# Linear attention, Fourier mixing and feed-forward on one core: work emitted batch by batch with ranks, against one fixed software pipeline

## The chip, the cores and the metric

The kernel runs on one core of a Trainium2 chip. The metric is device time in microseconds of one launch, and lower is better. Of each version several runs are timed; one more execution is recorded by the profiler, and the views of the profile come from it.

## The reference

Inputs are `r`, `k`, `v` of 4 batches x 8 heads x 768 positions x 48 (float32), a decay `w` and a bonus `u` of 8 x 48, and two feed-forward weights of 384 x 1536 and 1536 x 384. The first half is a linear attention with a decaying state, the second a Fourier mixing with a feed-forward layer:

```python
for t in range(S):
    cur = np.einsum('bhd,bhe->bhde', u[None] * kt, vt)
    y[:, :, t] = np.einsum('bhd,bhde->bhe', rt, state + cur)
    state = w[None, :, :, None] * state + np.einsum('bhd,bhe->bhde', kt, vt)
...
X = np.fft.fft(np.fft.fft(x, axis=1), axis=2)      # x: y with the heads side by side, 4 x 768 x 384
u = x + np.real(X)
un = (u - mean(u)) / np.sqrt(var(u) + 1e-06)       # over the last axis
out = u + np.maximum(un @ w_ch1, 0.0) @ w_ch2
```

## The kernel before, in words

The 768 positions of a batch are cut into 6 chunks of 128 positions, so there are 24 chunks. A batch goes through three functions.

`attention(b, ins)` (L181) runs the 6 chunks of a batch. For each chunk VectorE multiplies keys and queries by powers of the decay into `KR` (L191), ScalarE casts the values to `V` (L196), TensorE transposes `KR` in eight parts into PSUM (`tp`, L202), ScalarE copies that to `KRT` (L204), and VectorE makes the product `PR` (L206). TensorE then makes the 128 x 128 scores of all heads into two PSUM tiles `A_ps` (L212). The first is masked by VectorE (L218), the second is cast by ScalarE (L222) and masked by GpSimd (L223). `yd_ps` collects the output: a bonus per head (L229), the old state (L233), and scores times values (L243); ScalarE copies the bonus (L236), GpSimd multiplies it with `V` (`TT`, L238), and VectorE adds both into `X` (L255). The state is carried from chunk to chunk: TensorE makes `u_ps` (L248, L251), VectorE multiplies it by the decay into `Sst` (L253). After the chunks `fold` (L263) makes sums and differences of the batch's two halves on VectorE (`EO`, `XF`).

`fourier(b, X, XF)` (L271) does the transform over the positions with tables in 18 matmuls (L280), copied out by ScalarE (L282), and a mirrored copy `TR` on VectorE (L285). Then, for each of two halves of 384 positions and each of three blocks, six matmuls with `hid_t` make the second transform (L299, L301, L303); VectorE adds `X` (`UF`, L305) and takes the statistics (L308, L309). Per half ScalarE makes the root (L311) and the normalised `UN` (L318), and a transposing DMA on SP's queue writes `UNT` (L320), which is the input of the feed-forward layer.

`mlp(b, sh, UF, UNT)` (L325) does the feed-forward layer of one half: 12 groups of three matmuls with `W1` (L330), each cast by a ReLU on ScalarE into `HT` (L332), then three groups of 12 matmuls with `W2` (L336), to which VectorE adds `UF` (L339); GpSimd's queue writes the result out (L341). Over the program L330 and L336 have 288 matmuls each. Fourier and feed-forward share three PSUM buffers named `mm`.

What sets the order: the functions are Python that emits instructions; a planner then gives each engine a list, taking at each point of its own estimated time the ready instruction of best rank, and the engine runs this list. Rank is the order of emission, except that what stands in the `tc.high_priority(offset=5000)` block of the last loop (L350) is ranked 5000 places earlier. In that block stand the Fourier of batch `b`, the attention of batch `b + 1` and the loads of batch `b + 2`; the feed-forward of batch `b - 1` is emitted behind it at ordinary rank. The planner also hands out the buffers, and puts in the waits. `sp(...)` (L162) keeps an instruction behind everything emitted before it on its engine, and all loads and transposes of SP's queue go through it, so SP's queue has the order of emission: the loads of batch 0, the tables, the loads of batch 1, the two transposes of batch 0, the loads of batch 2, the transposes of batch 1, and so on. A load of a chunk is three DMAs of 192 KB (L171, L172, L175); the input pool holds 6 chunks. The weights are six DMAs on GpSimd's queue (L154, L156), put behind the `TT` of chunk 2 by `issue_after`.

Of the kernel before, what the change touches and what calls it, by code (L numbers as in the profile page):

```python
# [15 lines left out]
B = 4  # L16
H = 8
# [45 lines left out]
def kernel(  # L63
# [62 lines left out]
    NB = 3  # L126
# [24 lines left out]
    def load_weights():  # L151
        with tc.issue_after(marks["tt2"].ins):
            for dt in range(3):
                nc.gpsimd.dma_start(out=W1[:, dt, :], in_=w1[dt * 128:(dt + 1) * 128, :])  # L154
            for fg in range(3):
                nc.gpsimd.dma_start(out=W2[:, fg * 4:(fg + 1) * 4, :],  # L156
                                    in_=w2[fg * 512:(fg + 1) * 512, :].rearrange("(f p) d -> p f d", p=128))

    count = [0]
# [5 lines left out]
    def loads(b):  # L165
        ins = []
        for q in range(NQ):
            sl = slice(q * 128, (q + 1) * 128)
            kr = inp.tile([128, 2, H, D], F32, name="kr")
            vt = inp.tile([128, H, D], F32, name="vt")  # L170
            sp(nc.sync.dma_start(out=kr[:, 0], in_=k[b, :, sl, :].rearrange("h p d -> p h d")))  # L171
            sp(nc.sync.dma_start(out=kr[:, 1], in_=r[b, :, sl, :].rearrange("h p d -> p h d")))  # L172
            if b == 0 and q == 0:
                sp(nc.sync.dma_start(out=ident, in_=id_c.ap()))
            sp(nc.sync.dma_start(out=vt, in_=v[b, :, sl, :].rearrange("h p d -> p h d")))  # L175
            if b == 0 and q == 0:
                sp(nc.sync.dma_start(out=mtri, in_=mtri_c.ap()))
            ins.append((kr, vt))
        return ins

    def attention(b, ins):  # L181
        X = bp.tile([128, NQ, DM], BF16, name="X")
        EO = bp.tile([128, 2, 3, DM], BF16, name="EO", bufs=1)
        XF = bp.tile([128, 2, 3, DM], BF16, name="XF")
        Sst = None
        for q in range(NQ):
            i = count[0]
            count[0] += 1
            kr, vt = ins[q]
            KR = KRs[i % NB]  # L190
            nc.vector.tensor_tensor(  # L191
                out=KR.rearrange("t s p (a d) -> t (s p) a d", a=2)[:, :, :, 0:D],
                in0=kr.rearrange("t s (p a) d -> t (s p) a d", a=2),
                in1=wtab.rearrange("t s (p a d) -> t (s p) a d", a=2, d=D), op=AluOp.mult)
            V = wp.tile([128, H, D], BF16, name="V")
            cv = nc.scalar.copy(V, vt)  # L196
            if i == 0:
                tc.keep_in_program_order(cv)
            tp = ps.tile([128, 2, NP, 128], BF16, name="tp", bufs=1)
            for s in range(2):  # L200
                for p in range(NP):
                    nc.tensor.transpose(tp[:, s, p, :], KR[:, s, p, :], ident)  # L202
            KRT = wp.tile([128, 2, NP, 128], BF16, name="KRT")
            nc.scalar.copy(KRT, tp)  # L204
            PR = wp.tile([128, NP, 128], BF16, name="PR")
            nc.vector.tensor_tensor(out=PR, in0=KRT[:, 0], in1=KRT[:, 1], op=AluOp.mult)  # L206

            A_ps = [ps.tile([128, NP, 128], F32, name="A_ps", bufs=2) for _ in range(2)]
            for p in range(NP):
                for a in range(2):  # L210
                    rows = slice(a * 64, a * 64 + 64)
                    nc.tensor.matmul(A_ps[a][:, p, :], lhsT=KRT[rows, 0, p, :], rhs=KRT[rows, 1, p, :],  # L212
                                     start=(p == 0), stop=(p == NP - 1), skip_group_check=True)
            MAs = []
            for a in range(2):
                MA = wp.tile([128, NP, 128], BF16, name="MA", bufs=6)
                if a == 0:
                    nc.vector.tensor_tensor(out=MA, in0=A_ps[a], in1=mtri.unsqueeze(1).to_broadcast([128, NP, 128]),  # L218
                                            op=AluOp.mult)
                else:  # L220
                    AC = wp.tile([128, NP, 128], BF16, name="AC", bufs=2)
                    nc.scalar.copy(AC, A_ps[a])  # L222
                    nc.gpsimd.affine_select(out=MA, in_=AC, pattern=[[0, NP], [1, 128]], base=0,  # L223
                                            channel_multiplier=-1, compare_op=AluOp.is_gt, fill=0.0)
                MAs.append(MA)
            yd_ps = ps.tile([128, DM + H], F32, name="yd_ps", bufs=1)
            y_ps = yd_ps[:, 0:DM].rearrange("t (h d) -> t h d", h=H)
            for p in range(NP):
                nc.tensor.matmul(yd_ps[:, DM + 2 * p:DM + 2 * p + 2], lhsT=PR[:, p, :], rhs=UW[:, p, :],  # L229
                                 start=(p == 0), stop=False, skip_group_check=True)  # L230
# [26 lines left out]
            if b == 0 and q >= 3:  # L257
                fold(X, EO, XF, q - 3, q - 2)
# [131 lines left out]
```

## Time and profile before

| | us |
|---|---|
| median of 3 runs (lowest, highest) | 245.33 (243.44, 245.98) |
| profiled execution, its own time | 246.25 |
| its span, first to last instruction | 244.5 |
| TensorE busy (PE) | 192.5 |
| VectorE busy (DVE) | 131.8 |
| ScalarE busy (ACT) | 128.5 |
| GpSimd busy (POOL) | 59.8 |

The DMA queues moved 25.33 MB, of which the queue of SP's loads 17.96 MB. Times in the views are microseconds from the start of the span. PE is TensorE's matmuls, PEld its weight loads, SPq and POOLq the queues of SyncE and GpSimd. A row of a timeline has the start, the length, the engine, the line of the kernel, the operation, the tile written and those read, and how often; in brackets stands the idle time ahead of it and what ended that. The granted clock is the share of TensorE's full clock. "x24" is a count.

### The profile page before, as it was taken

Reading aid. Unit: us, or ns where it says so; the run is one execution under the profiler, and the core shown is the slowest. Engines: PE = TensorE matmul, PEld = TensorE weight load, DVE = VectorE, ACT = ScalarE, POOL = GpSimd, SP = SyncE. Lnnn points to the kernel's source line nnn. Section 1 sums busy time; section 2 is a strip of 40 time slices with the busy share of each in tenths; the row PEclk is TensorE's granted clock in tenths of the full one; section 3 lists DMA queues with packets and bytes.
Section 4 is the critical chain, followed back from the end, with each engine's and each line's share of the span. In section 5 each row is a group of like instructions: output and inputs, shape, how many; then the busy total and the mean of one; then the engine's idle time right before and its main releaser. Section 6 shows DMA issues by size and latency. Waiting matters only on the chain.

```text
span 244.5 us, 4268 instructions
## 1 busy us (share of the span) xinstructions
PE 192.5 (79%) x1640; PEld 122.4 (50%) x1640; DVE 131.8 (54%) x278; ACT 128.5 (53%) x255; POOL 59.8 (24%) x87
## 2 busy tenths in 40 slices
PE   0369760892869579987889899879999699999991
PEld 0256530471657466644555555446656356566560
DVE  3488970689878889693477686802028401011010
ACT  4646510547676445469278824590842955453620
POOL 4046740013233454020154430002010001010111
PEclk9999999998575555999999999999999999999999
DMA  6999999998699900005999200051010322020101
GB/s 115 186 186 214 249 189 192 183 186 121 122 191 171 165 4 0 1 3 99 215 229 190 46 32 35 12 117 64 35 66 0 82 49 97 3 97 31 67 35 64
DMA packets 88917, 25.33 MB, mean 104 GB/s; under 512 B 85312, under 2 KB 86976, under 8 KB 88896
## 3 DMA queue, kind: packets, MB, share of 16 engines
q1 hardware_dynamic: 85216, 17.96, 45.5%
q0 software_dynamic: 3680, 7.08, 11.1%
q8 instruction: 13, 0.21, 0.4%
q14 instruction: 8, 0.07, 0.1%
HBM read 20.32 MB, written 4.72 MB: 102 GB/s over the span
## 4 chain that ended last, share of the span: by engine, by line
issue 39%; PE 18%; DMA 11%; DVE 11%; POOL 8%; ACT 7%; SPq 4%; POOLq 0%; ACTq 0%; DVEq 0%
DMA kr<-in_r_dram 11%; POOL out_dram L341 4%; PE tp L202 4%; DVE KR L191 3%; PE A_ps L212 3%; POOL TT L238 3%; PE mm L280 2%; DVE PR L206 2%; ACT KRT L204 2%; ACT UN L318 1%; ACT HT L332 1%; PE u_ps L248 1%; POOL MA L223 1%; DVE MA L218 1%; PE mm L330 1%
## 5 line engine op out<-in xcount | busy, mean ns | idle before, releaser
L332 ACT ACTIVATE HT<-mm 128x384 bf16<-128x384 f32 x96 | 45.2, 490 | 25.2 <-PE mm L330 25.1
L330 PE MATMUL mm<-UNT,W 128*128 128x384 bf16 x288 | 52.3, 326 | 7.3 <-ACT HT L332 5.3
L336 PE MATMUL mm<-W,HT 128*128 128x384 bf16 x288 | 51.6, 326 | 0.0
L339 DVE TENSOR_TENSOR osb<-mm,UF 128x384 f32<-128x384 f32 x24 | 13.3, 553 | 64.4 <-PE mm L336 64.4
L330 PEld LDWEIGHTS <-W 128*128 128x128 bf16 x288 | 27.5, 98 | 26.1 <-issue 9.5
L202 PE MATMUL tp<-ident,KR 128*128 128x128 bf16 x192 | 22.6, 280 | 21.5 <-DVE KR L191 21.5
L341 POOL DMA_DIRECT2D out_dram<-osb x24 | 13.1, 548 | 100.1 <-DVE osb L339 100.1
L336 PEld LDWEIGHTS <-HT 128*128 128x128 bf16 x288 | 27.7, 98 | 16.9
L191 DVE TENSOR_TENSOR KR<-kr,wtab 128x768 bf16<-128x768 f32 x24 | 26.4, 1099 | 16.1 <-DMA kr<-in_r_dram 16.1
L223 POOL TENSOR_SCALAR_AFFINE_SELECT MA<-AC 128x512 bf16<-128x512 bf16 x24 | 17.2, 718 | 56.5 <-ACT AC L222 27.8
L202 PEld LDWEIGHTS <-KR 128*128 128x128 bf16 x192 | 16.4, 127 | 26.5 <-DVE KR L191 25.5
L204 ACT COPY KRT<-tp 128x1024 bf16<-128x1024 bf16 x24 | 24.3, 1012 | 9.9 <-PE tp L202 9.7
L238 POOL TENSOR_TENSOR TT<-V,DE 128x384 bf16<-128x384 bf16 x24 | 23.2, 968 | 23.3 <-ACT DE L236 23.2
L222 ACT CAST AC<-A_ps 128x512 bf16<-128x512 f32 x24 | 14.1, 586 | 18.7 <-PE A_ps L212 18.7
L196 ACT CAST V<-vt 128x384 bf16<-128x384 f32 x24 | 12.2, 511 | 18.5 <-DMA vt<-in_v_dram 17.9
L282 ACT CAST TT<-mm 128x386 bf16<-128x386 f32 (+1 forms) x24 | 13.4, 596 | 12.3 <-PE mm L280 11.9
L212 PE MATMUL A_ps<-KRT 64*128 64x128 bf16 x192 | 15.5, 270 | 4.5 <-ACT KRT L204 4.1
L255 DVE TENSOR_TENSOR X<-yd_ps,TT 128x384 bf16<-128x384 f32 x24 | 13.2, 550 | 9.5 <-POOL TT L238 8.1
L218 DVE TENSOR_TENSOR MA<-A_ps,mtri 128x512 bf16<-128x512 f32 x24 | 16.3, 682 | 0.7 <-PE A_ps L212 0.6
L318 ACT ACTIVATE UN<-UF,nm,rstd 128x384 bf16<-128x384 f32 x24 | 15.2, 701 | 1.9 <-DVE nm L314 1.9
L212 PEld LDWEIGHTS <-KRT 64*128 64x128 bf16 x192 | 8.4, 113 | 12.0 <-ACT KRT L204 9.4
L243 PE MATMUL yd_ps<-V,MA 128*128 128x48 bf16 x192 | 11.3, 202 | 3.6 <-POOL MA L223 1.2
(64 smaller groups left out, 236.1 us busy)
## 6 DMA issues: line engine op xcount, KB each, us to landing
kr<-in_k_dram SPq DMA_DIRECT2D x24, 192.0 KB, 4.5
kr<-in_r_dram SPq DMA_DIRECT2D x24, 192.0 KB, 4.6
vt<-in_v_dram SPq DMA_DIRECT2D x24, 192.0 KB, 4.6
out_dram<-osb POOLq DMA_DIRECT2D x24, 192.0 KB, 2.1
W<-in_moe_w_ch_dram POOLq DMA_DIRECT2D x6, 384.0 KB, 9.9
hid_t<-hid_c SPq DMA_DIRECT2D x1, 576.0 KB, 7.7
te_t<-te_c SPq DMA_DIRECT2D x1, 289.5 KB, 4.5
to_t<-to_c SPq DMA_DIRECT2D x1, 288.0 KB, 4.1
```

The costliest lines, as they stand in the source:

```text
L191: nc.vector.tensor_tensor(out=KR.rearrange("t s p (a d) -> t (s p) a d", a=2)[:, :, :, 0:D], in0=kr.rearrange("t s (p a) d -> t (s p) a d" ...
L202: nc.tensor.transpose(tp[:, s, p, :], KR[:, s, p, :], ident)
L204: nc.scalar.copy(KRT, tp)
L212: nc.tensor.matmul(A_ps[a][:, p, :], lhsT=KRT[rows, 0, p, :], rhs=KRT[rows, 1, p, :], start=(p == 0), stop=(p == NP - 1), skip_group_check ...
L218: nc.vector.tensor_tensor(out=MA, in0=A_ps[a], in1=mtri.unsqueeze(1).to_broadcast([128, NP, 128]), op=AluOp.mult)
L223: nc.gpsimd.affine_select(out=MA, in_=AC, pattern=[[0, NP], [1, 128]], base=0, channel_multiplier=-1, compare_op=AluOp.is_gt, fill=0.0)
L238: marks["tt%d" % i] = nc.gpsimd.tensor_tensor(out=TT, in0=V, in1=DE.unsqueeze(2).to_broadcast([128, H, D]), op=AluOp.mult)
L318: nc.scalar.activation(out=UN[:, j, :], in_=UF[:, j, :], func=Act.Identity, scale=rstd[:, j:j + 1], bias=nm[:, j:j + 1])
L330: nc.tensor.matmul(hp, lhsT=W1[:, dt, ft * 128:(ft + 1) * 128], rhs=UNT[:, :, dt, :], start=(dt == 0), stop=(dt == 2))
L332: nc.scalar.activation(out=HT[:, ft, :], in_=hp, func=Act.Relu)
L336: nc.tensor.matmul(op, lhsT=HT[:, ft, j * 128:(j + 1) * 128], rhs=W2[:, ft, :], start=(ft == 0), stop=(ft == 11))
L341: nc.gpsimd.dma_start(out=out[b, row:row + 128, :], in_=osb)
```

## The change: what it does

The three functions are cut into pieces that a single loop over steps emits, at ordinary rank everywhere; the rank is thus the order of this loop. Attention of a chunk becomes `phase1` (KR, V, transposes, KRT, PR), `phase2` (scores, masks, the state) and `phase3` (the output, `TT`, `X`, `fold`), and step `s` emits phase 1 of chunk `s`, phase 2 of chunk `s - 1`, phase 3 of chunk `s - 2`. `fourier` becomes a generator that yields after each of its six transform groups and after each of its six blocks; it is advanced three times a step, by three pieces each while `s < 12` and by one after that. The feed-forward work is a list `M` of 120 pieces (`mlp1`: one group of three matmuls and its ReLU; `mlp2`: twelve matmuls and an output), of which each step from `s = 10` on takes 2, 2 and 1, as far as the half that the next piece reads has been emitted. When the chunks are done the last Fourier pieces alternate with single feed-forward pieces, and the rest of `M` follows.

Besides: the loads are emitted one chunk a step, four chunks ahead, six of them at the start; W1 goes behind the `TT` of chunk 2 and W2 behind that of chunk 6; in batch 0 both masks go by ScalarE and GpSimd; the groups of the first transform go by column block outside and parity inside, with the mirrored copy behind each block; there are 4 `KR` buffers (3 before), 4 of `V`, `KRT`, `PR` and `Sst` (3 before), and 5 of `UF` and `UNT` (6 before).

```diff
-    NB = 3
+    NB = 4
...
-    def load_weights():
-        with tc.issue_after(marks["tt2"].ins):
+    def load_w1():
+        with tc.issue_after(marks[2].ins):
             for dt in range(3):
                 nc.gpsimd.dma_start(out=W1[:, dt, :], in_=w1[dt * 128:(dt + 1) * 128, :])
+
+    def load_w2():
+        with tc.issue_after(marks[6].ins):
             for fg in range(3):
...
-                if a == 0:
+            if a == 0 and b > 0:
...
-        for par in range(2):
-            for cb in range(3):
+        for cb in range(3):
+            for par in range(2):
...
+                yield
             nc.vector.tensor_copy(TR[:, cb, :, :], TT[:, cb, :, 384:0:-1])
...
-            UF = bp.tile([128, 3, DM], F32, name="UF", bufs=6)
-            UNT = bp.tile([128, 3, 3, 128], BF16, name="UNT", bufs=6)
+            UF = bp.tile([128, 3, DM], F32, name="UF", bufs=5)
+            UNT = bp.tile([128, 3, 3, 128], BF16, name="UNT", bufs=5)
...
+                if j < 2:
+                    yield
...
-            halves.append((UF, UNT))
-        return halves
+            bat[b]["halves"].append((UF, UNT))
+            yield
...
+    M = []
+    for hf in range(2 * B + 1):
         for j in range(3):
+            if hf < 2 * B:
+                M += [(mlp1, hf, ft) for ft in range(4 * j, 4 * j + 4)]
+            if hf > 0:
+                M += [(mlp2, hf - 1, j)]
+
+    def feed(n):
+        for _ in range(n):
+            if M and len(bat[min(M[0][1] // 2, B - 1)].get("halves", [])) > M[0][1] % 2:
+                f, hf, j = M.pop(0)
+                f(hf, j)
+
+    def advance(g, n):
+        for _ in range(n):
+            if next(g, "end") == "end":
+                return False
+        return True
+
+    INP = 6
+    for i in range(INP):
+        load(i)
     load_tables()
-    xs = [attention(0, ins)]
-    load_weights()
-    ins = loads(1)
-    hs = []
-    for b in range(B + 1):
-        with tc.high_priority(offset=5000):
-            if b < B:
-                hs.append(fourier(b, *xs[b]))
-            if b + 1 < B:
-                xs.append(attention(b + 1, ins))
-            if b + 2 < B:
-                ins = loads(b + 2)
-        if b > 0:
-            for sh in range(2):
-                mlp(b - 1, sh, *hs[b - 1][sh])
+    FG = None
+    MSTART = 10
+    for s in range(NC + 2):
+        if s < NC:
+            phase1(s)
+        if INP <= s + INP - 2 < NC:
+            load(s + INP - 2)
+        if FG:
+            FG = FG if advance(FG, 3 if s < 12 else 1) else None
+        if s >= MSTART:
+            feed(2)
+        if 1 <= s < NC + 1:
+            phase2(s - 1)
+        if FG:
+            FG = FG if advance(FG, 3 if s < 12 else 1) else None
+        if s >= MSTART:
+            feed(2)
+        if s >= 2:
+            phase3(s - 2)
+            if s - 2 == 2:
+                load_w1()
+            if s - 2 == 6:
+                load_w2()
+        if FG:
+            FG = FG if advance(FG, 3 if s < 12 else 1) else None
+        if s >= MSTART:
+            feed(1)
+        if s >= 2 and (s - 2) % NQ == NQ - 1:
+            FG = fourier((s - 2) // NQ)
+    while FG:
+        FG = FG if advance(FG, 1) else None
+        feed(1)
+    feed(len(M))
```

More of the change, by code (lines that the diff above doesn't have):

```diff
@@ L163, in sp @@
         return tc.keep_in_program_order(ins)
[L165 to L208, printed above, removed]
-            for p in range(NP):
[L210 to L214, printed above, removed]
-            for a in range(2):
-                MA = wp.tile([128, NP, 128], BF16, name="MA", bufs=6)
-                if a == 0:
[L218 to L227, printed above, removed]
```

184 lines of the change are left out of this document (128 added, 56 removed).

## The prediction

> **What bounds the kernel now.** First the page: totals and the row of the granted clock.
>
> ```profile
> span 244.5 us, 4268 instructions
> PE 192.5 (79%) x1640; PEld 122.4 (50%) x1640; DVE 131.8 (54%) x278; ACT 128.5 (53%) x255; POOL 59.8 (24%) x87
> ...
> PEclk9999999998575555999999999999999999999999
> ```
>
> TensorE is the busiest engine with 192.5 us, yet 52 us of the span it stands, and for six or seven slices (61 to 98 us) it runs at half its clock. Which stages those are, the view by stretches tells (columns: length, busy time and count of PE, PEld, DVE, ACT, POOL, then granted clock, DMA share, GB/s).
>
> ```profile
> 14.00:44.00 30.00, 17.34 (x188) 11.88 (x186) 20.75 (x36) 10.57 (x20) 13.87 (x18) 1.00 1.19 204
> ...
> 56.00:60.00 4.00, 1.13 (x24) 0.80 (x24) 3.89 (x12) 3.11 (x8) 1.46 (x2) 0.95 0.62 85
> 60.00:64.00 4.00, 2.49 (x20) 1.66 (x22) 3.63 (x6) 3.31 (x5) 0.00 (x0) 0.50 0.41 78
> ...
> 72.00:98.00 26.00, 20.32 (x231) 15.52 (x231) 22.31 (x35) 13.89 (x27) 11.73 (x14) 0.54 0.58 90
> ...
> 118.00:144.00 26.00, 23.29 (x286) 14.05 (x285) 18.28 (x32) 17.57 (x36) 11.81 (x16) 1.00 0.83 146
> 144.00:200.00 56.00, 50.60 (x320) 29.89 (x319) 23.05 (x63) 31.23 (x64) 4.73 (x9) 1.00 0.20 54
> 200.00:239.30 39.30, 39.29 (x242) 23.45 (x240) 6.12 (x11) 17.38 (x36) 5.94 (x11) 1.00 0.14 51
> ```
>
> There are four stages. From 14 to 44 us the DMA engines are full (share 1.19) and PE works 17 of 30 us. From 56 to 98 us attention runs alone, at a clock of 0.5. From 118 us PE has feed-forward work beside attention (23.29 of 26 busy). The last 39.3 us are 242 feed-forward matmuls and nothing else, 39.3 / 242 = 0.1624 us each. The 576 of the whole program (288 each of L330 and L336) are so worth 93.6 us, and the question is when the first of them runs. The timeline of PE says it, and gives durations:
>
> ```profile
> 44.02 1.03 PE L202 MATMUL tp<-ident,KR 128*128 128x128 bf16 x8 [8.78 <-DVE KR L191]
> ...
> 46.70 2.92 PE L280 MATMUL mm<-to_t,XF 128*128 128x384 bf16 x9
> ...
> 99.43 1.62 PE L280 MATMUL mm<-to_t,XF 128*128 128x384 bf16 x9
> ...
> 101.25 0.34 PE L299 MATMUL mm<-hid_t,TT 128*128 128x384 bf16 x1
> ...
> 103.23 0.33 PE L299 MATMUL mm<-hid_t,TR 128*128 128x384 bf16 x1
> ...
> 105.73 0.49 PE L330 MATMUL mm<-UNT,W 128*128 128x384 bf16 x2
> ...
> 120.17 0.62 PE L202 MATMUL tp<-ident,KR 128*128 128x128 bf16 x8 [0.74 <-DVE KR L191]
> ```
>
> Feed-forward starts at 105.73 us. Why so late? The timeline of SP's queue and the DMA list (last column: us to landing) show that its input was there long before:
>
> ```profile
> 49.41 0.94 SPq L171 DMA_DIRECT2D kr<-in_k_dram  x1
> ...
> 52.50 0.96 SPq L171 DMA_DIRECT2D kr<-in_k_dram  x1
> ...
> 58.87 5.26 SPq L320 DMA_TRANSPOSE UNT<-UN  x2
> ...
> 81.80 0.91 SPq L175 DMA_DIRECT2D vt<-in_v_dram  x1
> ...
> 109.86 4.78 SPq L320 DMA_TRANSPOSE UNT<-UN  x2
> ```
>
> ```profile
> UNT<-UN SPq DMA_TRANSPOSE x8, 3.3
> ```
>
> The first transpose of batch 0 is issued at 58.87 and lands 3.3 us later, at about 62. So some 43 us pass in which the feed-forward of batch 0 could fill the holes of attention and doesn't; it stands behind batch 1's Fourier in PE's order. Also, SP issues no load from 82.7 to 114.6: the loads of batch 3 stand behind batch 1's transposes.
>
> **The change, part by part.** I take the time as: start of feed-forward, plus the PE work that is left then, plus the tail.
>
> *The weights.* W1 and W2 are now issued apart. The two lines' rows and the chain:
>
> ```profile
> L154 POOL DMA_DIRECT2D W<-in_moe_w_ch_dram x3: 546/570/599, 22.7 to 25.1; - x3
> ...
> DMA to landing us min/median/max: 7.8/9.2/9.4
> ```
>
> ```profile
> L156 POOL DMA_DIRECT2D W<-in_moe_w_ch_dram x3: 784/789/794, 26.9 to 31.0; - x3
> ...
> DMA to landing us min/median/max: 10.3/11.4/11.6
> ```
>
> ```profile
> 23.86 19.05 DMA kr<-in_r_dram
> ```
>
> W1's last part lands at 25.1 + 9.4 = 34.5, W2's at 31.0 + 11.6 = 42.6, and the r half of chunk 6, issued at 23.86, only at 42.9, just after W2. The weights win against the loads. With W2 moved behind chunk 6's product, chunk 6 should land right after W1, about 36 us. After that a chunk takes 52.50 - 49.41 = 3.1 us, so chunk 12 would come 18.6 us later, plus the 8 us (34.5 to 42.6) that W2 now takes in this stretch: 63 us. The same bytes move; W2's 8 us come back. What is gained is that Fourier of batch 0, which stood behind chunk 6's transposes (the 8.78 us of idle before 44.02), starts earlier. But its DMA transposes stand on SP behind chunk 12's loads, which are issued about 5 us before they land, so at 58 to 60. That is where they are now. First feed-forward matmul: 60 + 3.3 = **63 us** (58 if the loads get more of the bandwidth, 67 if W2 starves them fully). It needs no wait of its own on W2: 16 first-layer pieces come before the first second-layer piece in the list.
>
> *The interleaving.* Up to 63 us the chunks come 3.1 us apart, so 12 have landed and about 11 are done. Left are 13 chunks of attention, three batches of Fourier, the 576 matmuls.
>
> Price of a chunk with feed-forward beside it: in 118 to 144 us the six chunks of batch 3 ran whole, and L330 and L336 in that stretch were
>
> ```profile
> 118.00:144.00 26.00, 8.31 (x36) 3.11 (x36) 1.00 0.83 146
> ```
>
> ```profile
> 118.00:144.00 26.00, 7.31 (x38) 3.18 (x37) 1.00 0.83 146
> ```
>
> so 74 matmuls, 12.0 us. (26 - 12.0) / 6 = 2.33 us a chunk. From below: PE's busy time alone, (23.29 - 12.0) / 6 = 1.88. From above, attention alone at half clock, by VectorE's starts of batch 2's first and sixth chunk:
>
> ```profile
> 71.07 0.95 DVE L191 TENSOR_TENSOR KR<-kr,wtab 128x768 bf16<-128x768 f32 x1
> ...
> 93.18 0.95 DVE L191 TENSOR_TENSOR KR<-kr,wtab 128x768 bf16<-128x768 f32 x1
> ```
>
> 22.1 / 5 = 4.42 us. I take 2.33, since the mixture there is the one that the change makes everywhere: 13 x 2.33 = **30.3 us**.
>
> Price of a batch of Fourier: from below, two groups of nine L280 at 1.62, and three blocks of the second transform from 101.25 to 103.23, so 6 x 0.66: 3.24 + 3.96 = 7.2 us. From above, 144 to 200 us held two batches and
>
> ```profile
> 144.00:200.00 56.00, 19.09 (x108) 10.49 (x108) 1.00 0.20 54
> ```
>
> ```profile
> 144.00:200.00 56.00, 19.28 (x104) 9.82 (x103) 1.00 0.20 54
> ```
>
> 212 feed-forward matmuls, 34.4 us: (56 - 34.4) / 2 = 10.8. There ScalarE had the normalisation and the ReLU at once. Spread over four steps this should be about halved: 8.9 between the two, 3 x 8.9 = **26.7 us**.
>
> *The end.* By the fixed pattern 73 of 120 pieces are emitted when attention ends, 13 more beside Fourier of batch 3, and 34 remain. From half 0's normalisation to the first piece that needs it there are five pieces and half a second transform, 4 x 0.49 + 12 x 0.1624 + 2.0 = 5.9 us, against
>
> ```profile
> L318 ACT ACTIVATE UN<-UF,nm,rstd 128x384 bf16<-128x384 f32 x24 | 15.2, 701 | 1.9 <-DVE nm L314 1.9
> ```
>
> 3 x 0.70 + 3.3 = 5.4 us and a few hand-overs: **1 us** lost, 6 at most. The tail behind the last matmul stays: 244.5 - 239.3 = **5.2 us**.
>
> *What costs nothing here.* In batch 0 the first mask moves from VectorE to ScalarE and GpSimd:
>
> ```profile
> L223 POOL TENSOR_SCALAR_AFFINE_SELECT MA<-AC 128x512 bf16<-128x512 bf16 x24 | 17.2, 718 | 56.5 <-ACT AC L222 27.8
> ...
> L222 ACT CAST AC<-A_ps 128x512 bf16<-128x512 f32 x24 | 14.1, 586 | 18.7 <-PE A_ps L212 18.7
> ...
> L218 DVE TENSOR_TENSOR MA<-A_ps,mtri 128x512 bf16<-128x512 f32 x24 | 16.3, 682 | 0.7 <-PE A_ps L212 0.6
> ```
>
> 6 x 0.586 = 3.5 us more on ACT and 4.3 us on POOL, 4.1 us less on DVE. In 14 to 44 us ACT is busy 10.57 and POOL 13.87 of 30, and the loads set the pace; without that cover it would be 3.5 us. The fourth KR buffer and the deeper V, KRT, PR pools only free chunks to overlap. UF and UNT lose a buffer; half 5 takes that of half 0, whose pieces end in step 15, seven steps earlier. Loads now go out four chunks ahead, one per step, so batch 3's no longer stand behind the transposes of batch 1; with steps of about 7 us that is hidden.
>
> *Clock.* The price of 2.33 holds at full clock (eight transposes in 0.62 us at 120.17; 1.03 at 44.02). The clock row has 0.95 in 56 to 60 us, where PE is busy 1.13 of 4, and 0.50 after; it comes back only with the Fourier matmuls near 98 us. Nine L280 at 46.70 took 2.92 us, twice the time at 99.43, though the row still says full there, so I trust spacings more. The Trainium skill (TensorE: Matmul & The Clock Gate, section "HAM oscillation — how this bites in real kernels") says that a gap of more than some 3.4 us between bursts puts PE back to half clock. That speaks against this pattern in one place: steps 15 and 16 get 2 and 1 pieces in place of 5, since batch 1's halves aren't ready. By the rule the sum would grow by 2 x (4.42 - 2.33) = 4.2 us; by the row of 118 to 144 us by nothing.
>
> Sum: 63 + 30.3 + 26.7 + 93.6 + 1 + 5.2 = 219.8 us of span. The profiled execution took 246.25 us, 1.75 more than its span: 221.6. The median of the runs, 245.33, is 0.4% under that execution, so **221 us**.
>
> **The rivals.**
>
> *Nearly no holes.* Feed-forward at 58 us, chunk at 1.88, Fourier at 7.2, nothing lost at the end: 58 + 24.4 + 21.6 + 93.6 + 5.2 = 202.8, with 0.85 for the rest of the way **204 us**. For: the last stage has no idle at all. Against: no mixed stage of this trace reached it.
>
> *Feed-forward still late.* Emission is only rank; if what kept it behind batch 1's Fourier is the planner's view of when its input is there, it starts at 105.73 again, with 7 chunks and two Fourier batches left: 105.7 + 16.3 + 17.8 + 93.6 + 5.2 = 238.6, so **239 us**. For: its input lay there 43 us unused while PE had holes. Against: it was emitted last.
>
> *PE's queue stands for late transposes (the slower one).* The 8.78 us before 44.02 are a wait of PE's transposes for a transfer, and the L280 matmuls listed behind them didn't pass. Now first-layer pieces stand among attention's instructions; where the real DMA transposes come later than planned, attention stands too. Four waits of 8.78 us, for the halves of batches 0 and 1 whose transposes meet a full DMA queue: 221 + 35 = **256 us**. It turns the gain from 24 us on, 6 us a half. Against: in 118 to 144 us PE lost only 2.7 of 26.
>
> *The planner makes almost the same order*, the change doesn't do what it says: 245 us. Against: the rank of 576 matmuls against attention is turned round.
>
> **How the numbers follow.** The forecast, 0.57 (its own range 212 to 231: start 58 to 67, Fourier 7.2 to 10.8, a starved clock 4.2); nearly no holes 0.12; still late 0.17; slower 0.09; same order 0.05. A measurement of this kernel can tell about 1% from no change. Faster by over 1%: 0.57 + 0.12 and 0.15 of the late case (its end above 242.9 is no change): 0.84; within 1%: 0.05 + 0.02 = 0.07; slower 0.09. The range for 8 in 10 takes the forecast, half of the case without holes and most of the late case: 206 to 240.
>
> **What would show it.** Right: first L330 at 58 to 67 us; granted clock 1.00 from there; no long stretch of SP without a load before all 24 chunks are in; PE busy over 88% from then to the end; last chunk's product near 160 to 170 us. Wrong: L330 first near 100 us; idle of PE's transposes or of L330 put down to DMA transposes or to UN for more than 10 us; a clock of 0.5 again after 70 us; PE idle for several us near the start of batch 3's feed-forward.

## The result, and the profile after

The changed kernel takes 235.07 us (median of 4 runs, 234.15 to 235.59), the kernel before 245.52 us beside it; the ratio is 0.9586, 95% interval 0.9523 to 0.9649. It is faster, by 10.4 us. The forecast was 221 us, 24 less than before. The span of the profiled execution is 233.5 us where the sum gave 219.8, and the 13.7 us between them are what the rest of this document looks for.

The page of the changed kernel, totals and granted clock:

```profile
span 233.5 us, 4269 instructions
...
PE 191.2 (82%) x1640; PEld 122.3 (52%) x1640; DVE 131.1 (56%) x273; ACT 129.3 (55%) x261; POOL 64.1 (27%) x93
...
PEclk9999999999599988995599999995699999999998
```

TensorE's busy time is what it was. The clock is up for most of the span now, but it falls four times, near 58, 85, 106 and 157 us. When does feed-forward run? The timeline of PE (L353 is the first layer, L362 the second):

```profile
63.73 2.57 PE L353 MATMUL mm<-UNT,W 128*128 128x384 bf16 x11
...
93.06 2.11 PE L362 MATMUL mm<-W,HT 128*128 128x384 bf16 x12
...
112.79 1.12 PE L353 MATMUL mm<-UNT,W 128*128 128x384 bf16 x3
...
149.55 2.11 PE L362 MATMUL mm<-W,HT 128*128 128x384 bf16 x12
...
162.85 1.12 PE L353 MATMUL mm<-UNT,W 128*128 128x384 bf16 x3 [0.22 <-DMA UNT<-UN]
```

It starts at 63.73 us, 42 us sooner than before. But no feed-forward matmul starts between the end of the group at 93.06 and 112.79, nor between that of 149.55 and 162.85: two dry stretches. The view by stretches (length, busy time and count of PE, PEld, DVE, ACT, POOL, clock, DMA share, GB/s), cut at their edges:

```profile
64.30:95.00 30.70, 28.53 (x251) 17.36 (x249) 19.25 (x31) 22.23 (x47) 8.90 (x10) 0.93 0.98 165
95.00:113.60 18.60, 16.12 (x208) 11.77 (x207) 16.53 (x35) 11.99 (x24) 7.90 (x11) 0.79 0.24 51
113.60:151.50 37.90, 35.25 (x270) 21.59 (x269) 20.41 (x42) 21.53 (x45) 6.33 (x10) 0.97 0.37 71
151.50:163.00 11.50, 6.03 (x101) 4.71 (x100) 6.01 (x13) 4.74 (x11) 5.24 (x7) 0.75 0.18 43
...
174.00:228.30 54.30, 53.43 (x337) 32.14 (x334) 16.30 (x38) 27.79 (x57) 7.04 (x13) 1.00 0.21 61
```

In the two dry stretches the clock is 0.79 and 0.75, in the second PE is busy 6.03 of 11.50; in the other three PE is busy for about 93% of the time or more. And the loads: SP's queue still waits behind transposes (87.97 is the last load DMA of chunk 20, 110.16 the first of chunk 21):

```profile
87.97 0.59 SPq L180 DMA_DIRECT2D vt<-in_v_dram  x1
108.73 1.34 SPq L339 DMA_TRANSPOSE UNT<-UN  x1
110.16 0.53 SPq L176 DMA_DIRECT2D kr<-in_k_dram  x1
...
125.43 1.29 SPq L339 DMA_TRANSPOSE UNT<-UN  x1
```

How many products of chunks were done when feed-forward began, the row of L271 (the last sum of a chunk) up to 64.3 us says:

```profile
0.00:64.30 64.30, 4.96 (x9) 0.95 1.08 190
```

Nine, not eleven: the last one at 62.2 us. (Products are counted from 1; chunks, as in the code, from 0, so product 9 ends chunk 8.)

Theory A from this: the list of feed-forward pieces runs dry, since the halves of the next batch are ready too late, and what runs alone there is slow. Theory B: the loads of chunks 21 to 23, held behind transposes, delay batch 3. Beside them stands the question of what each part of the change gave.

### The profile page after: what moved, and what is told of

The parts are those of the page before. It is cut to its first block, busy times and chain, and to the rows that moved or that the text cites. A ratio compares the mean times of both kernels' runs of the same rounds, so it can differ in the third digit from the quotient of the medians.

```text
span 233.5 us, 4269 instructions
## 1 busy us (share of the span) xinstructions
PE 191.2 (82%) x1640; PEld 122.3 (52%) x1640; DVE 131.1 (56%) x273; ACT 129.3 (55%) x261; POOL 64.1 (27%) x93
## 4 chain that ended last, share of the span: by engine, by line
issue 29%; PE 22%; ACT 11%; DMA 11%; POOL 9%; DVE 8%; SPq 6%; POOLq 0%; ACTq 0%; DVEq 0%
PE mm L353 6%; PE mm L362 5%; DMA vt<-in_v_dram 5%; DMA kr<-in_r_dram 5%; POOL TT L264 4%; POOL out_dram L367 3%; ACT KRT L203 3%; PE tp L201 3%; ACT HT L355 2%; ACT UN L337 2%; POOL MA L227 2%; SPq L176 2%; PE mm L298 2%; PE A_ps L216 2%; DMA UNT<-UN 2%
## 5 line engine op out<-in xcount | busy, mean ns | idle before, releaser
L355 ACT ACTIVATE HT<-mm 128x384 bf16<-128x384 f32 x96 | 46.0, 497 | 35.1 <-PE mm L353 34.7
L353 PE MATMUL mm<-UNT,W 128*128 128x384 bf16 x288 | 59.2, 341 | 2.7 <-DMA UNT<-UN 1.7
L362 PE MATMUL mm<-W,HT 128*128 128x384 bf16 x288 | 51.4, 331 | 0.0
L353 PEld LDWEIGHTS <-W 128*128 128x128 bf16 x288 | 28.3, 101 | 21.2 <-issue 4.8
L362 PEld LDWEIGHTS <-HT 128*128 128x128 bf16 x288 | 28.6, 99 | 19.5 <-issue 1.6
L227 POOL TENSOR_SCALAR_AFFINE_SELECT MA<-AC 128x512 bf16<-128x512 bf16 x30 | 22.2, 751 | 40.1 <-ACT AC L226 35.5
L264 POOL TENSOR_TENSOR TT<-V,DE 128x384 bf16<-128x384 bf16 x24 | 22.6, 941 | 36.4 <-ACT DE L262 34.2
L190 DVE TENSOR_TENSOR KR<-kr,wtab 128x768 bf16<-128x768 f32 x24 | 23.7, 991 | 12.9 <-DMA kr<-in_r_dram 12.9
L201 PE MATMUL tp<-ident,KR 128*128 128x128 bf16 x192 | 20.0, 258 | 12.3 <-DVE KR L190 11.5
L201 PEld LDWEIGHTS <-KR 128*128 128x128 bf16 x192 | 15.0, 116 | 15.4 <-DVE KR L190 13.4
L216 PE MATMUL A_ps<-KRT 64*128 64x128 bf16 x192 | 15.4, 257 | 9.0 <-ACT KRT L203 4.4
L226 ACT CAST AC<-A_ps 128x512 bf16<-128x512 f32 x30 | 17.2, 592 | 9.9 <-PE A_ps L216 9.8
L271 DVE TENSOR_TENSOR X<-yd_ps,TT 128x384 bf16<-128x384 f32 x24 | 13.3, 553 | 14.8 <-POOL TT L264 14.4
L337 ACT ACTIVATE UN<-UF,nm,rstd 128x384 bf16<-128x384 f32 x24 | 15.2, 697 | 3.6 <-DVE nm L333 3.5
L216 PEld LDWEIGHTS <-KRT 64*128 64x128 bf16 x192 | 8.5, 108 | 15.5 <-issue 7.4
L205 DVE TENSOR_TENSOR PR<-KRT 128x512 bf16<-128x512 bf16 x24 | 11.3, 471 | 8.5 <-ACT KRT L203 8.4
```

The source lines that it names most:

```text
L190: nc.vector.tensor_tensor(out=KR.rearrange("t s p (a d) -> t (s p) a d", a=2)[:, :, :, 0:D], in0=kr.rearrange("t s (p a) d -> t (s p) a d" ...
L264: marks[i] = nc.gpsimd.tensor_tensor(out=TT, in0=V, in1=DE.unsqueeze(2).to_broadcast([128, H, D]), op=AluOp.mult)
L337: nc.scalar.activation(out=UN[:, j, :], in_=UF[:, j, :], func=Act.Identity, scale=rstd[:, j:j + 1], bias=nm[:, j:j + 1])
L353: nc.tensor.matmul(hp, lhsT=W1[:, dt, ft * 128:(ft + 1) * 128], rhs=UNT[:, :, dt, :], start=(dt == 0), stop=(dt == 2))
L355: nc.scalar.activation(out=HTs[hf][:, ft, :], in_=hp, func=Act.Relu)
L362: nc.tensor.matmul(op, lhsT=HTs[hf][:, ft, j * 128:(j + 1) * 128], rhs=W2[:, ft, :], start=(ft == 0), stop=(ft == 11))
```

## The experiments

The runs are called e1 to e12.

### Feed-forward that never waits

All pieces read the halves of batch 0 (e1):

```diff
-        UF, UNT = bat[hf // 2]["halves"][hf % 2]
+        UF, UNT = bat[0]["halves"][hf % 2]
...
-            if M and len(bat[min(M[0][1] // 2, B - 1)].get("halves", [])) > M[0][1] % 2:
+            if M:
```

(The same in `mlp2`.)

> The feed-forward pieces of all batches read the normalised input and the residual of batch 0, so they never wait for a later half; feed takes a piece whenever the list has one. Nothing else changes and the amount of work is the same; the output of batches 1 to 3 is not the reference's. Theory A (the list runs dry: feed-forward stops twice, at 95 to 113 and 152 to 163 us of the changed kernel, attention alone is a chain of waits and the clock falls): both stretches vanish, the granted clock stays at 1.00 after 66 us, and about 14 us less, so 221 us. Theory B (the loads of chunks 21 to 23 stand behind transposes on SP's queue and batch 3's attention comes late): the loads stay where they are and the end comes at most 2 us sooner, 233 us.

227.48 us, ratio to before 0.9271 (0.9221 to 0.9321); span 225.3. Its stretches, the whole of feed-forward first, then the two that were dry:

```profile
64.40:220.10 155.70, 142.91 (x1220) 89.76 (x1218) 86.27 (x175) 92.45 (x193) 37.87 (x52) 0.98 0.39 82
95.00:113.60 18.60, 18.60 (x198) 12.82 (x198) 15.03 (x33) 12.40 (x26) 5.92 (x9) 1.00 0.16 44
151.50:163.00 11.50, 11.27 (x118) 7.68 (x116) 8.94 (x23) 7.42 (x16) 3.90 (x6) 1.00 0.24 61
```

```profile
63.77 1.96 PE L353 MATMUL mm<-UNT,W 128*128 128x384 bf16 x9
```

The work is the same, PE is full in both stretches, the clock is 1.00, and 8.2 us of span are gone (7.6 us by the medians, 235.07 and 227.48). The first late load, that of chunk 21, still leaves only at 112.45. So running dry costs 8 us, not the 14 that I expected. What is left is a check of the prices: from 63.8 to the last matmul at 220.1 are 156.3 us, and 15 chunks, three Fourier batches and 576 matmuls are, at the predicted prices, 35.0 + 26.7 + 93.6 = 155.3. (The 1 us lost at the end can't arise in this run, where no piece waits for a late half.) But 15 is the number of products that were missing; of two of these chunks TensorE had done most already, as the last part shows, so this is a rough check, good to some 4 us.

### The transposes on another queue

The transposes are issued from ScalarE's queue (e3):

```diff
-            sp(nc.sync.dma_start_transpose(out=UNT.rearrange("p j c t -> p (j c) t"),
+            sp(nc.scalar.dma_start_transpose(out=UNT.rearrange("p j c t -> p (j c) t"),
```

> The eight DMA transposes are issued from ScalarE's queue, so that no load stands behind one on SP's queue; nothing else changes. Theory B (loads behind transposes): the loads of chunks 21 to 23 leave 20 to 40 us sooner, batch 3's attention comes forward, and 6 to 12 us less: 223 to 229 us. Theory A (list runs dry): the loads come sooner, but feed-forward still stops at the same two places, within 2 us of 235, or some us worse since ScalarE now waits to issue.

237.67 us, 0.9667 (0.9622 to 0.9712). The loads were free, the k half of the last chunk is issued at 95.44, not at 129.97; the two stretches, now at 98 and 153 us, are as they were:

```profile
95.44 0.57 SPq L176 DMA_DIRECT2D kr<-in_k_dram  x1
```

```profile
98.00:116.80 18.80, 16.46 (x213) 12.10 (x211) 15.70 (x34) 12.50 (x25) 7.92 (x11) 0.82 0.28 59
153.50:165.00 11.50, 5.91 (x102) 4.58 (x100) 6.01 (x13) 4.74 (x11) 5.04 (x7) 0.83 0.18 43
```

Loads 34 us sooner bring nothing. Feed-forward even starts later, at 67.05, 3.3 us after the changed kernel's, and the span is 3.0 us longer. Theory B falls, though the wait is plain to see in the queue.

### The weights, put back and alone

W2 back behind chunk 2 in the changed kernel (e4):

```diff
-        with tc.issue_after(marks[6].ins):
+        with tc.issue_after(marks[2].ins):
...
-            if s - 2 == 6:
                 load_w2()
```

> W2 is issued together with W1 behind the product of chunk 2, as in the kernel before; all else as in the changed kernel. If moving W2 gives what the prediction said (chunk 6 lands some 7 us sooner, Fourier of batch 0 starts sooner, but feed-forward waits for the transposes anyway), feed-forward starts where it did, at 63 to 66 us, and the time is within 2 us of 235. If the early stage matters to the end, 3 to 7 us more: 238 to 242 us.

241.81 us, 0.9856 (0.9798 to 0.9914), 6.7 us more than with W2 moved. And the kernel before with W2 moved, nothing else (e5):

```diff
+    def load_w2():
+        with tc.issue_after(marks["tt6"].ins):
             for fg in range(3):
...
                 xs.append(attention(b + 1, ins))
+            if b == 0:
+                load_w2()
```

> The kernel before, with one part of the change alone: W2 is issued behind the product of chunk 6 instead of that of chunk 2; the order of all other work is the old one. Putting W2 back in the changed kernel cost 6.7 us. Theory W (most of the gain is the moved W2, the interleaving gives little): 237 to 240 us, so that 2 to 5 us are left for the interleaving. Theory I (the gain is the interleaving, and W2 only counts where feed-forward follows at once): within 2 us of 245.

241.20 us, 0.9824 (0.9749 to 0.9899). First feed-forward matmul with the weights together in the new order:

```profile
71.91 2.40 PE L353 MATMUL mm<-UNT,W 128*128 128x384 bf16 x7 [0.95 <-DMA UNT<-UN]
```

and with W2 moved in the old order:

```profile
97.67 1.34 PE L333 MATMUL mm<-UNT,W 128*128 128x384 bf16 x6
```

So moving W2 alone gives 1.8%, all the rest of the change without it 1.4%, both together 4.1%. Each of the two single gains is clear of zero by its interval, but they are not clear of each other; the other parts of the change were not undone one by one. In the new order W2's place moves the start of feed-forward by 8.2 us and the time by 6.7 (the spans of the profiled executions differ by 8.7, but that of this run took 243.91 us, the longest of the four): most of what starts feed-forward sooner there comes out at the end.

### Faster Fourier, and fewer pieces a step

Three Fourier pieces at each advance in all steps (e2):

```diff
-            FG = FG if advance(FG, 3 if s < 12 else 1) else None
+            FG = FG if advance(FG, 3) else None
```

> The Fourier pieces are advanced three at a time in every step, not only before step 12, so a batch's two halves are emitted within two steps rather than four; nothing else changes. Theory A (list runs dry): the halves are ready about 10 us sooner, feed-forward stops for shorter, and 5 to 9 us less: 226 to 230 us. Theory B (loads behind transposes): the transposes are emitted earlier between the loads, so they stand before more loads; no gain, 235 us or more.

241.66 us, 0.9814 (0.9760 to 0.9868): slower than the changed kernel, against my theory. The halves of batch 1 did come sooner, with transposes at 101.30 and 106.69 in place of 108.73 and 125.43, but the shortage moved to the end, where nothing is left to fill it:

```profile
201.71 1.14 PE L353 MATMUL mm<-UNT,W 128*128 128x384 bf16 x3 [7.74 <-DMA UNT<-UN]
```

The other way, four pieces a step, not five, with Fourier as it was (e6):

```diff
             phase2(s - 1)
...
         if s >= MSTART:
-            feed(2)
+            feed(1)
```

> From step 10 on each step takes four pieces of feed-forward (2, 1, 1) in place of five, so a batch's 27 to 30 pieces last seven steps, not five and a half; nothing else changes. Theory A (the list runs dry): feed-forward no longer stops for more than some 5 us in the two stretches, and the time comes near that of the run that never waits, 227.5: 227 to 231 us. If what is left at the end decides instead (pieces kept back only to run there at the same rate): within 2 us of 235.

231.93 us, 0.9436 (0.9351 to 0.9522). The second dry stretch is gone, the first is left (101 to 113 us):

```profile
101.00:113.00 12.00, 9.16 (x146) 7.01 (x144) 10.61 (x22) 8.88 (x18) 5.90 (x8) 0.90 0.32 62
113.00:163.00 50.00, 47.33 (x405) 29.39 (x406) 31.26 (x68) 29.25 (x64) 10.69 (x17) 0.96 0.36 73
```

Both, with Fourier fast for batches 0 and 1 only (`3 if s < 18 else 1`; e8):

> Four pieces of feed-forward a step as in e6, and the Fourier pieces advanced three at a time up to step 17, so for batches 0 and 1 (one at a time after that). In e6 one dry stretch was left, 101 to 113 us, before batch 1's first half. Theory A (the list runs dry): that stretch shrinks to some 5 us, and the time to 227 to 230 us. If the faster Fourier only shifts the shortage to the end as in e2: 232 us or more.

**229.39 us, 0.9330 (0.9296 to 0.9364): faster than both kernels.** Batch 1's halves come sooner (transposes at 98.05 and 103.63), and the first dry stretch is gone; the span is 227.4 us:

```profile
95.00:113.60 18.60, 16.88 (x176) 10.78 (x175) 13.51 (x30) 13.44 (x29) 6.97 (x8) 1.00 0.87 156
```

One stop is left: before 164.57 us PE stands 3.75 us for the sums that `fold` makes behind the last chunk, and no feed-forward piece runs between 160.6 and 165.5.

And three pieces a step up to step 15, four after that, on top of it (e9):

```diff
-        if s >= MSTART:
+        if s >= 16:
             feed(1)
```

> As e8, but three pieces a step in steps 10 to 15 and four after that, so that batch 0's pieces last longer. Theory A: the first dry stretch is gone, 226 to 229 us. If PE is then short of work between 66 and 95 us, where pieces are held back, within 1 us of e8 or above it.

231.40 us, 0.9432 (0.9388 to 0.9477): 2 us worse than the one before. From 63.8 to 95 us, where pieces are held back, PE is busy for 27.37 us, in the run before for 28.47; no piece runs between 75.2 and 85.4, nor between 118.3 and 125.4. Holding pieces back too long costs as running out does.

### What sets the pace in a dry stretch

Idle work for TensorE's clock in the dry stretches of the changed kernel (e7):

```diff
+        if i in (13, 14, 15, 16, 17, 20, 21, 22, 23):
+            with tc.issue_after(last.ins):
+                for n in range(3):
+                    wm = ps.tile([128, 384], F32, name="mm", bufs=3)
+                    for dt in range(3):
+                        nc.tensor.matmul(wm, lhsT=W1[:, dt, 0:128], rhs=W1[:, dt, 384:768],
+                                         start=(dt == 0), stop=(dt == 2))
```

> The changed kernel with idle work in the two dry stretches: behind the last matmul of chunks 13 to 17 and 20 to 23 three groups of three matmuls of W1 with itself, 27 groups or 81 matmuls, 13.2 us at full clock, whose result nobody reads. If half of the loss there is the fallen clock: the granted clock stays at 1.00, and the time is 232 to 236 us in spite of the added work. If only the chain of waits counts, with PE idle inside it: 235 to 238 us. If PE had no room there: 246 to 248 us.

246.74 us, 1.0091 (1.0054 to 1.0128), the last of my cases (PE had no room). Of 13.2 us of added matmuls 11.7 came out at the end. The clock rose from 0.79 to 0.92 in the first stretch, hardly in the second:

```profile
95.50:117.30 21.80, 19.49 (x245) 13.82 (x242) 16.33 (x35) 13.59 (x26) 8.30 (x11) 0.92 0.17 38
157.00:169.40 12.40, 7.34 (x109) 5.45 (x108) 5.55 (x13) 4.73 (x11) 4.94 (x7) 0.77 0.17 41
```

But the run doesn't test what it was made for. `issue_after` says after what an instruction may run, not when, and of the 81 idle matmuls only 18 ran in the first stretch and 9 in the second; 27 ran between the two and 27 after the second, where PE is nearly full and has to make room for them. In the first stretch 18 x 0.1624 = 2.9 us of idle work made it 3.2 us longer, in the second 1.5 us made it 0.9 longer. So in the first a better clock did not pay for the work; more the run doesn't say. To see the pace of a chunk by itself, the changed kernel without feed-forward (e10):

```diff
-                M += [(mlp1, hf, ft) for ft in range(4 * j, 4 * j + 4)]
+                M += []
...
-        nc.gpsimd.dma_start(out=out[b, row:row + 128, :], in_=osb)
+        nc.gpsimd.dma_start(out=out[b, row:row + 128, :], in_=UF[:, j, :])
```

> The changed kernel without the feed-forward layer: no piece of it is emitted, and what is written out is the residual sum alone, so the output is not the reference's; loads, attention, Fourier and transposes are as before. It gives the pace of a chunk that runs alone. If a chunk alone is a chain of waits (3.6 to 3.9 us between products in the dry stretches): the 18 chunks of batches 1 to 3 take over 65 us, product 24 stands near 115 to 125 us, and the span is 130 to 145 us. If a chunk alone goes at the 2.33 us that I took beside feed-forward: the loads' 3.1 us bind, product 24 comes near 105 us, span below 125 us.

157.77 us, span 156.0 (one execution, as in the next run): more than either guess, for attention and Fourier alone. Products 14 to 18, those of chunks 13 to 17 (the last two numbers are the starts of the first and the last), and what the engines did meanwhile:

```profile
L271 DVE TENSOR_TENSOR X<-yd_ps,TT x5: 527/551/558, 88.9 to 105.3; 128x384 bf16<-128x384 f32 x5
```

```profile
88.50:105.80 17.30, 12.72 (x171) 9.70 (x169) 16.54 (x41) 10.97 (x23) 9.82 (x15) 0.79 0.86 155
```

16.4 / 4 = 4.1 us from product to product, with VectorE busy 16.54 of 17.30, at a clock of 0.79. Fourier of batch 1 ran beside them; its second transform is worth 3.96 us a batch, with 12 matmuls of line L316, and L316 had in this stretch

```profile
88.90:105.30 16.40, 3.33 (x11) 0.97 (x10) 0.79 0.83 151
```

so 11/12 of it, 3.6 us, and a chunk alone is (16.4 - 3.6) / 4 = 3.2 us. This is an estimate, and a low one: it charges Fourier with PE's time, though VectorE was the fuller engine, and the last two spacings, which hold no second transform, are 3.47 and 3.57 us. The changed kernel's second dry stretch agrees, products 21 to 24 with next to no Fourier:

```profile
L271 DVE TENSOR_TENSOR X<-yd_ps,TT x4: 557/558/558, 153.1 to 163.0; 128x384 bf16<-128x384 f32 x4
```

9.9 / 3 = 3.3. The same with 12 idle matmuls, 2.0 us, behind each chunk from 9 on (e11):

```diff
+        if i >= 9:
+            with tc.issue_after(last.ins):
+                for n in range(4):
...
```

> The kernel of e10 (no feed-forward, its output is not the reference's) with idle work that holds TensorE's clock: behind the last matmul of each chunk from 9 on four groups of three matmuls of W1 with itself, 12 matmuls or 2.0 us at full clock a chunk, 180 in all, 29 us. In e10 products 13 to 17 came 4.1 us apart at a clock of 0.5 to 1. If the fallen clock is what makes a chunk alone slow: the clock stays up, the products come 3.1 to 3.5 us apart and the span is below e10's 156. If the chain of waits between engines is, and PE has room: 4 to 4.3 us apart, span 154 to 162. If PE's own work is: 6 us apart, span 180 or more.

170.24 us, span 168.5, between my cases:

```profile
L278 DVE TENSOR_TENSOR X<-yd_ps,TT x5: 540/544/558, 93.1 to 115.8; 128x384 bf16<-128x384 f32 x5
```

```profile
92.50:116.30 23.80, 21.17 (x244) 14.41 (x242) 20.89 (x46) 14.46 (x27) 9.12 (x14) 0.98 0.41 101
```

Of these 22.7 us a whole second transform takes 3.96, a group of the first 0.5, and the idle work, by its row,

```profile
93.10:115.80 22.70, 7.90 (x46) 3.96 (x45) 0.99 0.40 101
```

46 x 0.1624 = 7.5 us. (22.7 - 3.96 - 0.5 - 7.5) / 4 = 2.7 us a chunk. So the price of a chunk falls from 3.2 us alone to 2.7 with idle work beside it and 2.33 in the mixture. How much of the 0.5 is the clock (0.79 against 0.98), and how much is idle work that fits into PE's holes, these two runs can't tell apart. Last, VectorE's masks of batches 1 and 2 given to ScalarE and GpSimd in the changed kernel (e12):

```diff
-            if a == 0 and b > 0:
+            if a == 0 and b > 2:
```

> The changed kernel with the first mask on ScalarE and GpSimd in batches 0, 1 and 2, not in batch 0 alone: 12 masks of 0.68 us, 8 us in all, leave VectorE, 12 casts of 0.59 go to ScalarE and 12 selects of 0.75 to GpSimd; nothing else changes. In the first dry stretch (95 to 113.6 us) VectorE is busy 16.5 of 18.6. If VectorE sets the pace there: batch 1's and 2's chunks come closer together, the first stretch ends 2 to 4 us sooner, and the time is 231 to 233 us. If the chain of waits does (the select is on it, longer by 0.7 us and one engine more): 235 to 239 us.

235.55 us, 0.9578 (0.9506 to 0.9651), the time of the changed kernel. VectorE was relieved, 15.28 of 20.30 in the first dry stretch, but the stretch was no shorter:

```profile
95.00:115.30 20.30, 18.18 (x215) 12.51 (x212) 15.28 (x33) 13.78 (x29) 11.34 (x15) 0.69 0.22 47
```

The loads and VectorE's masks were each changed by themselves, and neither shortened a dry stretch. (VectorE isn't cleared by this alone: the select is longer than the mask that it replaces and stands in the chain, and the clock was lower, 0.69.)

The clock can be told apart from the rest, since the changed kernel and the one with the weights together run the same instructions in the same order on every engine in the first dry stretch. From product 15 to 16 and from 16 to 17 in the changed kernel, then from 16 to 17 with the weights together:

```profile
101.95:105.82 3.87, 2.96 (x47) 2.13 (x42) 3.61 (x12) 3.67 (x8) 1.42 (x2) 1.00 0.00 0
105.82:109.70 3.88, 2.79 (x32) 2.21 (x32) 3.35 (x7) 2.60 (x7) 1.50 (x3) 0.52 0.00 2
```

```profile
115.22:119.09 3.87, 2.26 (x32) 1.94 (x32) 3.34 (x6) 2.60 (x6) 1.49 (x3) 0.83 0.01 2
```

At a clock of 0.52 and of 0.83 the same step takes 3.88 and 3.87 us, so here the clock doesn't set the pace of a chunk. What does, the second stretch shows in the order of time:

```profile
157.68 1.90 ACT L337 ACTIVATE UN<-UF,nm,rstd 128x384 bf16<-128x384 f32 x3 [0.76 <-DVE nm L333]
...
159.49 0.14 ACT L262 COPY DE<-yd_ps 128x8 f32<-128x8 f32 x1
...
159.78 0.83 POOL L264 TENSOR_TENSOR TT<-V,DE 128x384 bf16<-128x384 bf16 x1 [2.15 <-ACT DE L262]
...
160.64 0.56 DVE L271 TENSOR_TENSOR X<-yd_ps,TT 128x384 bf16<-128x384 f32 x1 [2.40 <-POOL TT L264]
161.25 0.24 PE L255 MATMUL yd_ps<-UW,PR 128*128 128x2 bf16 x4 [1.09 <-DVE X L271]
...
161.93 0.17 ACT L262 COPY DE<-yd_ps 128x8 f32<-128x8 f32 x1 [2.30 <-PE yd_ps L259]
...
162.18 0.83 POOL L264 TENSOR_TENSOR TT<-V,DE 128x384 bf16<-128x384 bf16 x1 [1.56 <-ACT DE L262]
...
163.04 0.56 DVE L271 TENSOR_TENSOR X<-yd_ps,TT 128x384 bf16<-128x384 f32 x1 [1.84 <-POOL TT L264]
```

It is a ring of hand-overs. The kernel has one `yd_ps` (`bufs=1`), so the bonus of the next chunk (L255) waits for the product of the last (L271), and behind it come `DE` on ScalarE, `TT` on GpSimd and the product on VectorE, each waiting for the one before. The last round, from 161.25 to the end of the product at 163.60, takes 2.35 us with nothing in its way; in the round before, from 157.32, `DE` stood behind 1.90 us of normalisation on ScalarE, and it took 3.88. With feed-forward at hand PE fills these waits (e1: 11.27 of 11.50 us busy); without, it idles. In the first stretch the ring is there too, and in its step of 3.88 us `DE` again stands behind 1.90 us of normalisation, but VectorE is busy for 16.53 of 18.60 us beside it; which of the two sets the other steps there is not shown. No run gave `yd_ps` a second buffer.

The clock does cost something, but behind the stretches: when feed-forward is back, PE is full and the clock is still low.

```profile
112.79:117.20 4.41, 4.41 (x20) 2.58 (x20) 3.06 (x6) 1.43 (x4) 0.00 (x0) 0.61 0.48 88
162.85:167.30 4.45, 4.45 (x17) 2.33 (x17) 4.00 (x7) 1.08 (x3) 0.15 (x1) 0.50 0.02 4
```

Six matmuls of L353 in a row take 2.12 us at 165.04 and 1.14 at 120.47. As an estimate from these rows, 4.41 x 0.39 + 4.45 x 0.50 = 3.9 us are lost there, near half of the 8.2 that e1 gained; the other half is lost inside the stretches. No run raised the clock there and changed nothing else.

## Why the prediction was right or wrong

**The start of feed-forward: the number right, the reason wrong.** 63 us predicted, 63.73 measured; that they agree is luck. The prediction has the transposes wait on SP behind chunk 12's loads. Those were all issued by 58.1; the queue then stood until 59.55, when the normalisation (L337) was done on ScalarE:

```profile
57.11 0.98 SPq L180 DMA_DIRECT2D vt<-in_v_dram  x1
59.55 1.39 SPq L339 DMA_TRANSPOSE UNT<-UN  x1
```

```profile
55.04 0.51 ACT L195 CAST V<-vt 128x384 bf16<-128x384 f32 x1 [3.16 <-DMA vt<-in_v_dram]
...
57.62 1.90 ACT L337 ACTIVATE UN<-UF,nm,rstd 128x384 bf16<-128x384 f32 x3 [0.96 <-DVE nm L333]
```

ScalarE had stood 3.16 us for the values of chunk 10, a load issued at 44.22, just after the three parts of W2 (41.9 to 43.4), and 10.7 us on its way. With the weights together it is the same: the last load of chunk 12 is issued by 59.7, the transpose leaves at 68.51, behind a normalisation that ends at 68.48, and feed-forward starts at 71.91. So W2's place acts through Fourier and the normalisation, not through the loads of chunk 12. Chunk 6 was predicted at 36 us: its last load lands at 36.4, and its product with the decay starts at 34.90, before at 43.00.

**The chunks that are left: too few, by 1.5 to 4.7 us.** "12 have landed and about 11 are done" was an inference from the pace of the loads. Nine products were done. Counted so, the two missing chunks at 2.33 us are 4.7 us. But TensorE had made the transposes and scores of eleven chunks by then (88 matmuls each of L201 and L216, eight a chunk); what was missing of chunks 9 and 10 is the output part, L229, L233 and L243 of the kernel before, 26.5 of the 82.2 us that its attention lines have on PE. That is a third, so 1.5 us. What held the products back is again chunk 10's load: products 7 and 8 start at 42.09 and 59.09, Fourier of batch 0 fills PE up to 52 us, and then PE stands 3.45 us, until 56.52, for a `KRT` that ScalarE makes behind that load.

**The price of a chunk: near enough beside feed-forward, wrong as a price for all.** The step that failed is "I take 2.33, since the mixture there is the one that the change makes everywhere". The mixture is there in 156 us of e1, where the whole sum closes within some 4 us, but not in the two dry stretches of the changed kernel. I had counted the pieces and seen steps 15 and 16 short, but I took this for two steps and a question of the clock, 4.2 us at most. That count goes by the order in which the pieces are emitted, with batch 1's first half in step 16 and five pieces a step from step 17 on. In the run the transpose of this half was issued at 108.73 and its first piece ran at 112.79, after product 18, which step 19 emits: the next halves come only after a batch's whole attention and Fourier, and for 18.6 and 11.5 us attention and Fourier have nothing beside them. Measured, e1 against the changed kernel: 8.2 us, of which some 3.9 are the low clock behind the stretches.

So 8.2 of the 13.7 us are shown by e1. The other 5.5 are what e1's span, 225.3, has over the forecast's 219.8: 0.8 at the start and 5.7 of work, less the 1 us at the end that e1 can't lose. Of the 5.7 the chunks begun but not done are 1.5 to 4.7; the rest, 1.0 to 4.2, lies in the prices of a chunk (2.33) and of Fourier (8.9), which no run separates. Errors in them could cancel.

**The clock: one place right, the reason wrong.** It fell where batch 1's halves were late, as forecast, and where batch 2's were, which wasn't; two more falls lie elsewhere. The rule that I cited from the Trainium skill (TensorE: Matmul & The Clock Gate, section "HAM oscillation — how this bites in real kernels") asks for a gap of more than some 3.4 us between bursts. Only the first fall, near 58 us, has such a gap ahead of it, the 3.45 us before 56.52. At the third, that of the first dry stretch, it was not there. This is the changed kernel's stretch just before it, and the longest idle time of PE from 88 to 106 us:

```profile
102.00:106.00 4.00, 2.92 (x45) 2.13 (x42) 3.74 (x12) 3.79 (x8) 1.42 (x2) 0.99 0.00 0
```

```profile
104.93 0.38 PE L216 MATMUL A_ps<-KRT 64*128 64x128 bf16 x4 [0.61 <-DVE MA L222]
```

PE counted as busy 2.92 of 4 us with attention's short matmuls, never idle for more than 0.61 us, and the clock still went to half. I priced the fall by dearer chunks, 2 x (4.42 - 2.33) = 4.2 us, and left it out of the sum. The spacing of chunks didn't follow the clock (3.88 us at 0.52, 3.87 at 0.83); what the low clock cost were the feed-forward and Fourier matmuls behind the stretches, some 3.9 us. That the two figures are alike is chance. (In the kernel before, too, the clock came back sooner than the prediction says: 0.77 in 68 to 72 us, not only near 98.)

**The loads: wrong, and harmless.** "batch 3's no longer stand behind the transposes of batch 1" was wrong; chunk 21's load waited 20 us for one. e3 shows that it cost nothing: without the wait the dry stretches stay as they are.

**The rivals.** Feed-forward didn't start late, PE didn't lose time to late transposes (L353 waited 1.7 us for them in all), and the order did change. The forecast's own mechanism, feed-forward beside attention from 63 us on, held in the main, with a second half that I hadn't priced.

## What to carry to other kernels

A sum of PE work over a stage holds only while there is independent work to put beside a chain of small steps: count for each stretch not only how much filler there is, but when the next portion of it becomes ready, and what the chain costs alone (here, by estimate, 3.2 to 3.6 us a chunk alone, 2.33 in the mixture). Spending filler faster is not better; it has to last until the next portion, and some must be left for the last chain, so the rate at which it is given out and the rate of its producer are set together (e2, e6 and e8). And undo each part of a change alone: here a moved weight load, a detail beside the pipeline, was worth about as much as all the rest.

## What the runs showed of the hardware that was not expected

TensorE's granted clock went to 0.50 at 106 us although PE's longest idle time in the 18 us before was 0.61 us: being listed as busy 73% of the time with matmuls of mostly 2 to 128 columns didn't hold it. It came back only after some 3.4 us of full PE work at 112.79, and some 4.5 at 162.85. And the weights on GpSimd's queue crowd out the loads on SP's: with all six parts issued together, between 25.9 and 29.1 us, the k half of chunk 7, issued at 28.2, landed only at 45.3; with three, the same half issued at 27.7 landed at 37.2.
